# A band and strided attention feeding a GELU feed-forward layer: the start-up order written anew, with the residue mask and one exponential ahead of it

## The chip, the core and the metric

The kernel runs on one core of one Trainium2 chip. The core has a matrix engine (PE in the profile, with its weight loads as PEld), a vector engine (DVE), an activation engine (ACT), a general engine (POOL), a sequencer that issues the transfers (SP), and 16 DMA engines that carry them. The metric is the time of one launch in microseconds (us); less is better.

## The reference

Eight batches of eight heads, 576 tokens, head dimension 64. Heads 0 to 3 attend to a band of 32 tokens, heads 4 to 7 to all earlier tokens of the same residue modulo 32. The attention output, 4608 tokens of 512 channels, goes through a feed-forward layer with 2048 hidden units, all in float32:

```
rel = pos[:, None] - pos[None, :]
mask_local   = (rel >= 0) & (rel < 32)
mask_strided = (rel >= 0) & (pos[None, :] % 32 == pos[:, None] % 32)
scores = where(mask, (q @ k.T) / 8, -1e9)
attn   = softmax(scores);  x = attn @ v        # 4608 x 512
h = x @ w_in;  g = 0.5 * h * (1 + erf(h / sqrt(2)));  out = g @ w_out
```

## The kernel before

**Tiling.** The tokens are cut into 12 tiles of 384, the hidden units into 16 blocks of 128. One step n is one block for one tile: `ffn_h` (H of step n: 12 matmuls of 384 columns, lines 602 to 604), `ffn_g` (GELU and a cast on ACT, a subtraction on DVE, lines 611 to 615) and `ffn_o` (O of step n: 9 matmuls of 512 columns, lines 641 to 643). Every float32 product is made of three reduced ones, from a high and a low part of each operand: xh and xl of the tile, two parts of a weight block, gh and gl. There are 192 steps; steps 0 to 15 are those of tile 0, and tile 1 begins with step 16.

**Weights.** `load_w` brings block f as one transfer into a tile `ws`. `split_w` makes the two parts w from it in five pieces, which the order names with a c: a cast `lead` (line 150 on ACT or 148 on DVE, by `TOP_V`), an ACT piece (153), a DVE piece (155), the high part (161 on ACT or 159 on DVE, by `HIGH_V`) and the low part (163 on DVE).

**Attention of tile 0.** The band heads are three jobs L0 to L2 of 128 tokens (`local_job`: scores, a masked maximum on DVE at line 205, exponentials on ACT at 210, transposes, the product with v at line 263, and `to_x`, which writes xh on ACT at 230 and xl on DVE at 232). The strided heads of tile 0 are done on PE: two `half_tile` jobs (a and b; they need the residue mask `smask`, line 379) and one `strided_tile` job (A: line 413 on PE, four transposes on DVE at 418, casts on ACT at 421, subtractions on DVE at 424).

**Attention of tile 1.** The band heads are three jobs L3 to L5 (`band_job`): scores on PE (line 290), a masked maximum on DVE (304), exponentials on ACT (308), a normalization and a transpose on DVE (311 to 314), eight small transfers per job into a tile `first` (line 319, 16 KB each, issued by SP), the product with v on PE (328, written X_L) and `to_x`. The strided heads are done on DVE as "units" (u1): products of queries and keys, line 477, which come as a product and a read of its sum, and weighted sums at 517 and 519; their inputs are the tiles sq, sk and sv, loaded by the tokens E (sq and sk) and e (sv).

**What sets the order.** `START` lists the pieces up to step 15, one token per piece, and inside `manual_schedule` each of DVE, ACT, PE and SP runs its own pieces strictly in that order: w, q and v are loads of a weight block, of a job's queries and keys, and of its values; S and B load the strided inputs of tile 0 (qka and va); c, f, a, b, A and u advance a split, a step, a half tile, the strided tile, a unit; L advances a band job. POOL is not in that set: the scheduler orders its masks and fills. From step 16 on the order comes from `step(n)` and is the same in both kernels.

**Queues.** All transfers are issued by SP, in order. Each waits on the semaphore of the transfer eight places ahead of it, since eight semaphores go round; the first eight do not. So SP holds at most eight transfers in flight, and whatever stands behind one of them waits with it. A `first` transfer waits besides for the DVE transpose at line 314.

**Ahead of START** stand the masks on POOL (lines 691 to 712) and 50 small matmuls `lead_in` on zeros (line 684). The residue mask is made of four POOL instructions at line 712 and two DVE ones at 714 and 716, at the end of the masks.

Of the kernel before, what the change touches and what calls it, by code (L numbers as in the profile page):

```python
# [30 lines left out]
NGR = 16  # L31
# [19 lines left out]
    c0 c3 A0 w7 L2 A0 w5 L1 L2 L1 c3 c0 L3 L2 L1 v4 c0 A0 L1 L3 v5 c1 A0 L3 c3 f0 c1 w9 L3 c3 c1 c2 v3
    c3 c2 u1 c1 c4 f0 w6 c1 L4 w8 c2 f0 f1 c4 f0 c2 c7 w13 c4 c7 c2 f0 f1 c7 f1 c5 w14 f2 c4 e q5 c5 f1
    c4 f1 f2 c5 c7 u1 w10 f2 f3 c9 w11 c7 c9 L3 f2 f3 c5 f4 L3 c6 w12 f3 L3 c6 f3 f2 c5 f4 f4 c6 c8 w15
    f5 f4 c6 u1 c8 f3 c6 f5 c8 f5 c13 f6 f5 c13 c8 c9 f4 f6 f6 c8 c14 f7 f6 c14 c13 c9 c14 f5 c10 c9 c10
    f8 u1 f7 c10 f7 c13 f6 f7 c11 f8 f8 c13 f9 c11 f8 c10 c11 f7 c12 c10 c12 u1 f10 f9 c12 f9 c11 f9 f8
    L4 f10 f10 c11 u1 L5 f10 f9 c12 L4 L5 c12 f11 L5 u1 c14 L5 f10 f11 c14 f12 u1 f11 c15 f11 L4 L5 c15
    f13 u1 L5 f12 f12 L5 u1 f11 f13 f13 f12 f13 f14 u1 c15 f12 f14 f14 u1 c15 L4 f14 u1 f13 c15 L4 u1
    f15 L4 f14 f15 f15 f15 f15 f15
# [24 lines left out]
def attn_ffn_kernel(ctx: ExitStack, tc: tile.TileContext, qk, vl, qka, va, qs, ks, vs, w, out):  # L83
# [593 lines left out]


# [31 lines left out]
    for h in range(HL):  # L710
        m = smask[h * 32:(h + 1) * 32]
        nc.gpsimd.iota(m.bitcast(I32), pattern=[[-1, MA]], base=0, channel_multiplier=1)

    nc.vector.tensor_scalar(smask.bitcast(U32), smask.bitcast(U32), 0x80000000 | (STRIDE // NGR - 1), None,
                            ALU.bitwise_and)
# [201 lines left out]
```

## Time and profile before

| | |
|---|---|
| three timed runs | 881.61, 881.28, 881.52 us; median 881.52 us |
| the profiled execution | 880.11 us, of which 878.3 us are its span |
| PE busy in the span | 859.5 us of matmul, 771.0 us of weight loads |
| DVE, ACT, POOL busy | 704.0, 482.8, 17.4 us |
| mean granted PE clock | 0.992 |
| transfers | 66.67 MB, of which 16.8 MB are the 16 weight blocks |

A time in the profile counts from the start of the span. "Busy" is the sum of an engine's instructions, and the idle time before an instruction is put down to what released it. A tile's name carries no number in the profile, so H step 10 is the eleventh group of four instructions at line 602.

### The profile page before, as it was taken

What the parts mean: (1) busy time and instruction counts of PE and PEld (TensorE: products, weight loads), DVE (VectorE), ACT (ScalarE), POOL (GpSimd) and SP (SyncE); (2) the same over time, 40 slices, a digit from 0 to 9 for tenths busy, and PEclk for the clock granted to TensorE, in tenths of its full rate; (3) what the DMA queues carried; (4) which work ended last, traced back from release to release, by engine and by line L of the source; (5) the groups of instructions that cost most, each with busy time, mean ns of one, the idle gap of its engine ahead of it and who ended that gap; (6) DMA issues with size and microseconds to landing.
All of it is one profiled execution on the core that took longest, in us unless ns stands there. A gap on an engine that the chain in (4) does not pass through costs nothing.

```text
span 878.3 us, 19580 instructions
## 1 busy us (share of the span) xinstructions
PE 859.5 (98%) x6084; PEld 771.0 (88%) x6084; DVE 704.0 (80%) x4890; ACT 482.8 (55%) x990; POOL 17.4 (2%) x89
## 2 busy tenths in 40 slices
PE   7699999999999999999999999999999999999998
PEld 6598899989989989989998898988988988989997
DVE  5998899888898987798999979999799896751111
ACT  5898386259356357348547536636643743643222
POOL 5000100000000000000000000000000000000000
PEclk9699999999999999999999999999999999999999
DMA  9893220230220121121203112112012112000001
GB/s 311 302 387 121 87 79 19 82 110 20 82 82 15 60 91 58 34 79 39 86 3 114 33 57 85 44 51 106 19 56 90 41 34 65 9 11 7 29 1 37
DMA packets 34552, 66.67 MB, mean 76 GB/s; under 512 B 6800, under 2 KB 16528, under 8 KB 34448
## 3 DMA queue, kind: packets, MB, share of 16 engines
q1 hardware_dynamic: 34448, 65.43, 22.4%
q8 instruction: 48, 0.79, 0.4%
q14 instruction: 56, 0.46, 0.2%
HBM read 51.64 MB, written 9.44 MB: 70 GB/s over the span
## 4 chain that ended last, share of the span: by engine, by line
PE 95%; DVE 1%; POOL 1%; issue 1%; ACT 1%; SPq 0%; DMA 0%; POOLq 0%; ACTq 0%; DVEq 0%
PE H L602 16%; PE H L604 15%; PE O L642 15%; PE H L603 15%; PE O L643 15%; PE O L641 15%; PE X_L L328 2%; PE S_L L290 1%; SPq L319 0%; ACT PT_L L308 0%; PE S_L L254 0%; DVE w L163 0%; PE A L413 0%; DMA first<-PT_L 0%; POOL bmask L706 0%
## 5 line engine op out<-in xcount | busy, mean ns | idle before, releaser
L611 ACT ACTIVATE H<-H 128x384 f32<-128x384 f32 x192 | 91.3, 475 | 344.8 <-PE H L604 300.6
L602 PE MATMUL H<-xh,w 128*128 128x384 f32 x768 | 262.7, 342 | 1.2 <-ACT w L161 1.2
L604 PE MATMUL H<-xh,w 128*128 128x384 f32 x768 | 260.7, 339 | 0.9 <-DVE w L163 0.9
L603 PE MATMUL H<-xl,w 128*128 128x384 f32 x768 | 259.6, 338 | 0.6 <-DVE xl L424 0.6
L519 DVE SCALAR_TENSOR_TENSOR acc<-sv,sc,acc 128x64 f32<-128x64 f32 x1158 | 251.0, 283 | 0.5
L643 PE MATMUL O<-w,gl 128*128 128x512 f32 x576 | 228.2, 396 | 0.0
L642 PE MATMUL O<-w,gh 128*128 128x512 f32 x576 | 227.9, 396 | 0.0
L641 PE MATMUL O<-w,gh 128*128 128x512 f32 x576 | 224.6, 390 | 0.0
L477 DVE CUSTOM_DVE_ANT_0 junk<-sq,sk 128x64 f32<-128x64 f32 x1290 | 207.3, 224 | 2.7 <-issue 2.4
L615 DVE TENSOR_TENSOR gl<-H,gh 128x384 fp32r<-128x384 f32 x192 | 106.7, 556 | 109.8 <-ACT gh L613 109.6
L602 PEld LDWEIGHTS H<-xh,w 128*128 128x128 f32 x768 | 145.4, 189 | 10.7 <-ACT w L161 1.4
L603 PEld LDWEIGHTS H<-xl,w 128*128 128x128 f32 x768 | 145.1, 189 | 8.3 <-DVE xl L424 1.1
L604 PEld LDWEIGHTS H<-xh,w 128*128 128x128 f32 x768 | 145.1, 189 | 1.4 <-DVE w L163 1.4
L643 PEld LDWEIGHTS O<-w,gl 128*128 128x128 f32 x576 | 108.2, 188 | 23.1
L642 PEld LDWEIGHTS O<-w,gh 128*128 128x128 f32 x576 | 108.2, 188 | 18.0
L641 PEld LDWEIGHTS O<-w,gh 128*128 128x128 f32 x576 | 108.6, 189 | 17.4
L477 DVE DVE_READ_ACCUMULATOR2_ANT sc<- 128x1 f32 x1290 | 113.2, 88 | 0.0
L613 ACT CAST gh<-H 128x384 fp32r<-128x384 f32 x192 | 92.2, 480 | 6.0
L611 ACT ACT_TABLE_LOAD x60 | 77.0, 1283 | 1.1
L487 ACT ACT_TABLE_LOAD x35 | 44.9, 1283 | 0.6
L308 ACT ACTIVATE PT_L<-P_L,nm_L 128x64 f32<-128x64 f32 x132 | 44.3, 336 | 0.5 <-DVE nm_L L304 0.2
L308 ACT ACT_TABLE_LOAD x24 | 30.8, 1283 | 0.8 <-DMA band<-PT_L 0.3
(109 smaller groups left out, 489.6 us busy)
## 6 DMA issues: line engine op xcount, KB each, us to landing
ws<-in_w_dram SPq DMA_DIRECT2D x16, 1023.8 KB, 11.7
qk<-in_qk_dram SPq DMA_DIRECT2D x36, 320.0 KB, 4.6
out_dram<-ob SPq DMA_DIRECT2D x34, 256.0 KB, 2.6
vl<-in_vl_dram SPq DMA_DIRECT2D x36, 192.0 KB, 3.4
sk<-in_ks_dram SPq DMA_DIRECT2D x8, 576.0 KB, 4.9
sv<-in_vs_dram SPq DMA_DIRECT2D x8, 576.0 KB, 3.7
band<-PT_L SPq DMA_DIRECT2D x240, 16.0 KB, 1.8
sq<-in_qs_dram SPq DMA_DIRECT2D x4, 576.0 KB, 4.0
```

Of the source, the lines that this page charges most:

```text
L308: nc.scalar.activation(pv[:, :, h, :], p1[:, h * 2 * QB:(h + 1) * 2 * QB].rearrange("p (c t) -> p c t", c=2), AF.Exp, bias=nm[:, h:h + 1], ...
L477: nc.vector.tensor_tensor_reduce(junk, sq[vi, "q"][:, r0 + r, :], sq[vi, "k"][:, c, :], 1.0, 0.0, ALU.mult, ALU.add, ss[u][:, r, c:c + 1])
L519: nc.vector.scalar_tensor_tensor(acc[:, r, :], sq[vi, "v"][:, c, :], wgt, acc[:, r, :], ALU.mult, ALU.add)
L602: nc.tensor.matmul(hp, w1[f][:, 0, c, :], xh[:, c, :], start=(c == 0), stop=False)
L603: nc.tensor.matmul(hp, w1[f][:, 0, c, :], xl[:, c, :], start=False, stop=False)
L604: nc.tensor.matmul(hp, w1[f][:, 1, c, :], xh[:, c, :], start=False, stop=(c == NC - 1))
L611: nc.scalar.activation(hp, hp, AF.Gelu)
L613: nc.scalar.copy(gh, hp)
L615: nc.vector.tensor_tensor(gl, hp, gh.bitcast(F32), ALU.subtract)
L641: nc.tensor.matmul(o, gh[:, sl], w2[f][:, 0, :], start=(f == 0), stop=False)
L642: nc.tensor.matmul(o, gh[:, sl], w2[f][:, 1, :], start=False, stop=False)
L643: nc.tensor.matmul(o, gl[:, sl], w2[f][:, 0, :], start=False, stop=(f == NF - 1))
```

## The change

The list `START` is written anew, with other `TOP_V`, `HIGH_V` and `QUOT_V`. The residue mask moves from the end of the mask code to its head, on POOL and DVE. A tile `warm` of one column is zeroed by DVE, and ACT takes its exponential before anything else, so that the first table load of ACT stands there. The 50 `lead_in` matmuls become 18. The steps after 15 are not touched.

```diff
 START = """
-    q0 q2 S0 B0 q1 v0 v2 w0 L0 w3 v1 L2 L0 L0 L2 b0 q3 a0 L2 L0 b0 L0 b0 w1 b0 L0 a0 L1 L2 w2 a0 L2 a0
-    b0 L0 L1 a0 E b0 L0 w4 a0 L1 b0 L0 a0 b0 a0 b0 a0 b0 L2 L0 a0 c0 L1 q4 L2 b0 a0 L1 L0 c0 L1 A0 L1 L2
...
+    q0 q1 q2 S0 w0 w1 v0 B0 L0 v1 w3 L1 L0 L2 L0 L1 q5 L2 L1 L0 L0 L0 v2 b0 L2 L1 L1 a0 b0 b0 L1 L0 L2
+    b0 a0 L2 b0 a0 L1 L0 L2 w2 a0 L1 L2 b0 a0 c0 L2 a0 c0 b0 a0 b0 a0 q3 b0 a0 b0 c1 c0 w5 L0 a0 c1 b0
...
 """.split()
-TOP_V = [4, 6, 11]
-HIGH_V = [0, 2, 4, 5, 8, 12]
-QUOT_V = (1, 2)
+TOP_V = [0, 4, 5, 8]
+HIGH_V = [0, 2, 4, 5, 6, 13]
+QUOT_V = (0, 2)
...
+    for h in range(HL):
+        m = smask[h * 32:(h + 1) * 32]
+        nc.gpsimd.iota(m.bitcast(I32), pattern=[[-1, MA]], base=0, channel_multiplier=1)
+
+    nc.vector.tensor_scalar(smask.bitcast(U32), smask.bitcast(U32), 0x80000000 | (STRIDE // NGR - 1), None,
+                            ALU.bitwise_and)
+    nc.vector.tensor_scalar(smask, smask.bitcast(I32), 0, NEG, ALU.not_equal, ALU.mult)
+
+    warm = const.tile([P, 1], F32, name="warm")
+    nc.vector.memset(warm, 0.0)
+    nc.scalar.activation(warm, warm, AF.Exp)
 
     zero = const.tile([P, 32], F32, name="zero")
     nc.vector.memset(zero, 0.0)
     lead_in = ps_h.tile([P, TT], F32, name="lead_in", tag="H")
-    for i in range(50):
+    for i in range(18):
...
-    for h in range(HL):
-        m = smask[h * 32:(h + 1) * 32]
-        nc.gpsimd.iota(m.bitcast(I32), pattern=[[-1, MA]], base=0, channel_multiplier=1)
-
-    nc.vector.tensor_scalar(smask.bitcast(U32), smask.bitcast(U32), 0x80000000 | (STRIDE // NGR - 1), None,
-                            ALU.bitwise_and)
-    nc.vector.tensor_scalar(smask, smask.bitcast(I32), 0, NEG, ALU.not_equal, ALU.mult)
-
```

Three places show what the new list does. The first is SP's queue. Before, from the load of weight block 2 on (`ws_2`; the number behind a tile's name is its block or job, and the last number only counts tiles), these rows stand in it:

```order
L133 DMA ws_2_454<-in_w_dram 128x4095
L454 DMA sq_1_469<-in_qs_dram 128x256 x3
L454 DMA sk_1_473<-in_ks_dram 128x256 x3
L133 DMA ws_4_479<-in_w_dram 128x4095
L183 DMA qk_4_511<-in_qk_dram 128x640
L133 DMA ws_7_597<-in_w_dram 128x4095
L133 DMA ws_5_611<-in_w_dram 128x4095
L189 DMA vl_4_646<-in_vl_dram 96x512
L189 DMA vl_5_663<-in_vl_dram 96x512
L133 DMA ws_9_690<-in_w_dram 128x4095
L319 DMA first_0_283<-PT_L3_655 32x128 x8
L189 DMA vl_3_709<-in_vl_dram 96x512
```

Now, eleven weight blocks are issued first, and SP's queue goes on from the tenth and eleventh of them like this:

```order
L133 DMA ws_6_683<-in_w_dram 128x4095
L133 DMA ws_14_698<-in_w_dram 128x4095
L319 DMA first_2_258<-PT_L5_632 32x128 x8
L319 DMA first_1_256<-PT_L4_760 32x128 x8
L319 DMA first_0_254<-PT_L3_686 32x128 x8
L189 DMA vl_8_910<-in_vl_dram 96x512
L183 DMA qk_8_948<-in_qk_dram 128x640
L133 DMA ws_10_955<-in_w_dram 128x4095
L189 DMA vl_7_966<-in_vl_dram 96x512
L454 DMA sq_1_969<-in_qs_dram 128x256 x3
L454 DMA sk_1_973<-in_ks_dram 128x256 x3
L183 DMA qk_7_999<-in_qk_dram 128x640
```

All 24 `first` transfers stand together behind block 14; sq and sk of the units, which stood ahead of block 4, stand behind block 10, which itself stands behind the 24. Before, jobs L4 and L5 sent their 16 `first` transfers behind all weight blocks.

The second place is DVE ahead of step 0. Before, between the split of weight block 0 (tiles ws_0 and w_0) and the last xl of the band jobs:

```order
L155 SCALAR_TENSOR_TENSOR ws_0_306<-ws_0_306 128x1024
L418 STREAM_TRANSPOSE qka_0_295<-A0_0_387 128x256
L418 STREAM_TRANSPOSE qka_0_295<-A1_0_352 128x256
L418 STREAM_TRANSPOSE qka_0_295<-A2_0_523 128x256
L418 STREAM_TRANSPOSE qka_0_295<-A3_0_524 128x256
L159 CAST w_0_624<-ws_0_306 128x1024
L232 TENSOR_TENSOR xl_0_504<-S0_L2_325,xh_0_503 128x2x128
L163 TENSOR_TENSOR w_0_624<-ws_0_306,w_0_624 128x1024
```

Now, at the same place, DVE has:

```order
L159 CAST w_0_494<-ws_0_272 128x1024
L155 SCALAR_TENSOR_TENSOR ws_1_274<-ws_1_274 128x1024
L232 TENSOR_TENSOR xl_0_497<-S0_L0_279,xh_0_496 128x2x128
L163 TENSOR_TENSOR w_0_494<-ws_0_272,w_0_494 128x1024
L232 TENSOR_TENSOR xl_0_497<-S0_L1_296,xh_0_496 128x2x128
L163 TENSOR_TENSOR w_1_512<-ws_1_274,w_1_512 128x1024
L418 STREAM_TRANSPOSE qka_0_268<-A0_0_390 128x256
L418 STREAM_TRANSPOSE qka_0_268<-A1_0_351 128x256
L418 STREAM_TRANSPOSE qka_0_268<-A2_0_515 128x256
L418 STREAM_TRANSPOSE qka_0_268<-A3_0_516 128x256
L155 SCALAR_TENSOR_TENSOR ws_3_294<-ws_3_294 128x1024
L232 TENSOR_TENSOR xl_0_497<-S0_L2_313,xh_0_496 128x2x128
```

Blocks 0 and 1 are now both split before the strided transposes, and a piece of block 3 follows; before, block 1 was split only after the strided subtractions at line 424.

The third place is DVE around step 7, where the products of the units at line 477 (sc is their sum) now begin. Before, they began here, between the splits of blocks 3 and 1:

```order
L155 SCALAR_TENSOR_TENSOR ws_1_430<-ws_1_430 128x1024
L163 TENSOR_TENSOR w_3_704<-ws_3_321,w_3_704 128x1024
L477 ISA junk_3_3_0_719,sc_3_713<-sq_1_469,sk_1_473 128x64
L477 ISA sc_3_713 128x1
L477 ISA junk_4_3_0_721,sc_4_715<-sq_1_469,sk_1_473 128x64
```

Now they begin behind the low part of block 8, and this is where the first eight of them end:

```order
L477 ISA junk_4_3_1_1066,sc_4_1050<-sq_1_969,sk_1_973 128x64
L477 ISA sc_4_1050 128x1
L477 ISA junk_5_2_0_1068,sc_5_1052<-sq_1_969,sk_1_973 128x64
L477 ISA sc_5_1052 128x1
L155 SCALAR_TENSOR_TENSOR ws_10_955<-ws_10_955 128x1024
L615 TENSOR_TENSOR gl_7_1082<-H_7_1027,gh_7_1081 128x384
```

A piece of block 10 and gl of step 7 stand behind the eight products; 16 more products follow, and then the low part of block 10 (line 163).

More of the change, by code (lines that the diff above doesn't have):

```diff
@@ L48 @@
 START = """
-    q0 q2 S0 B0 q1 v0 v2 w0 L0 w3 v1 L2 L0 L0 L2 b0 q3 a0 L2 L0 b0 L0 b0 w1 b0 L0 a0 L1 L2 w2 a0 L2 a0
-    b0 L0 L1 a0 E b0 L0 w4 a0 L1 b0 L0 a0 b0 a0 b0 a0 b0 L2 L0 a0 c0 L1 q4 L2 b0 a0 L1 L0 c0 L1 A0 L1 L2
[L51 to L58, printed above, removed]
+    q0 q1 q2 S0 w0 w1 v0 B0 L0 v1 w3 L1 L0 L2 L0 L1 q5 L2 L1 L0 L0 L0 v2 b0 L2 L1 L1 a0 b0 b0 L1 L0 L2
+    b0 a0 L2 b0 a0 L1 L0 L2 w2 a0 L1 L2 b0 a0 c0 L2 a0 c0 b0 a0 b0 a0 q3 b0 a0 b0 c1 c0 w5 L0 a0 c1 b0
+    a0 q4 c0 L0 w7 c1 L1 L1 L0 c1 c0 A0 v4 A0 c3 L1 c1 c3 A0 L2 v5 L2 c3 w4 L5 A0 w8 L2 L5 c3 w9 A0 L3
+    c2 c3 c2 f0 w6 L3 L5 w14 c2 L3 L5 L4 f0 c2 f1 c5 c2 f0 c5 f0 L4 f0 f1 c5 f1 L4 c4 f2 c5 f1 c4 c5 L4
+    c7 f1 c4 f2 L3 f3 f2 c4 c7 f2 c4 f2 c6 c7 c6 f4 f3 c6 f3 c7 f3 L5 c6 c9 f3 c7 L5 c9 c6 f5 f4 L5 f4
+    c8 f4 c8 w10 L4 c9 E f5 f6 c8 L4 f5 c9 L4 f5 w11 f4 f6 c9 f6 c8 w13 f6 e f7 c10 c8 w15 w12 c10 u1 f5
+    v3 f7 c10 f7 c14 f8 f7 u1 c10 u1 c14 f6 f8 c10 c11 f9 u1 f8 c11 f8 u1 f7 f9 f9 c11 c13 f10 f9 c11
+    c14 c13 c11 f8 f10 c13 c12 f11 c12 c13 c13 f10 u1 f9 c12 f10 c12 u1 L3 f11 f10 c12 u1 f11 f12 L3 c14
+    f11 L3 u1 c15 f11 f12 c14 f12 c15 f13 f12 u1 c15 f12 f13 f13 u1 c15 f14 f13 u1 f13 f14 c15 f14 u1
+    f14 f15 u1 f14 f15 f15 f15 f15 f15
 """.split()
-TOP_V = [4, 6, 11]
-HIGH_V = [0, 2, 4, 5, 8, 12]
-QUOT_V = (1, 2)
+TOP_V = [0, 4, 5, 8]
+HIGH_V = [0, 2, 4, 5, 6, 13]
+QUOT_V = (0, 2)
 ROWS = [(vi, b, r) for vi, (b, r0, r1) in enumerate(VISITS) for r in range(r0, r1)]
```

## The prediction

> **What bounds the kernel now.** I read the chain of work that ended last first, then PE's waits, then PE's order of time, then stretches of the start.
>
> ```profile
> PE 95%; DVE 1%; POOL 1%; issue 1%; ACT 1%; SPq 0%; DMA 0%; POOLq 0%; ACTq 0%; DVEq 0%
> PE X_L L328 <- DMA first<-PT_L: 1.9, 1, 1.9
> 35.28 0.69 PE H L604
> 52.43 0.33 PE L602 MATMUL H<-xh,w 128*128 128x384 f32 x1
> 56.62 0.33 PE L602 MATMUL H<-xh,w 128*128 128x384 f32 x1
> 73.36 0.33 PE L602 MATMUL H<-xh,w 128*128 128x384 f32 x1
> 102.48 0.34 PE L602 MATMUL H<-xh,w 128*128 128x384 f32 x1
> ```
>
> 95% of the chain is PE. The third row, of the chain itself, is the third matmul of step 1. The four rows of matmuls are the first of H in steps 5, 6, 10 and 16: a step (H and one O) takes 56.62 - 52.43 = **4.19 us** when PE never waits. From step 16 on the order is the same in both kernels, and PE's only wait after that at 35.3 us is the 1.9 us for the `first` transfers of job L5, just ahead of step 13. So the time after step 16 is fixed, and the change is worth what it moves step 16, corrected for work that stands on the other side of it. Before, O of step 14 came behind H of step 16; in the changed order it comes ahead of it. O takes half a step, 2.1 us, so the moment to beat is 102.48 + 2.1 = 104.6.
>
> These are stretches of the start: the length, busy time and instructions of PE, PEld, DVE, ACT and POOL, the granted clock, the share of the DMA engines, GB/s.
>
> ```profile
> core 0: us, PE busy (x) PEld busy (x) DVE busy (x) ACT busy (x) POOL busy (x), PEclk, DMA share, GB/s
> 10.00:15.00 5.00, 2.93 (x39) 1.97 (x29) 3.19 (x19) 4.96 (x24) 3.15 (x15) 1.00 1.01 321
> 15.00:20.00 5.00, 4.60 (x92) 3.83 (x92) 4.52 (x18) 4.97 (x14) 0.00 (x0) 1.00 1.03 334
> 20.00:25.00 5.00, 2.76 (x125) 2.16 (x128) 4.31 (x9) 4.71 (x10) 0.00 (x0) 1.00 1.01 393
> 25.00:30.00 5.00, 4.16 (x37) 3.05 (x21) 4.47 (x17) 4.10 (x12) 0.00 (x0) 0.60 1.06 404
> 30.00:35.00 5.00, 1.69 (x34) 0.97 (x34) 5.00 (x21) 4.94 (x6) 0.00 (x0) 0.50 1.03 391
> 35.00:40.00 5.00, 4.72 (x14) 4.46 (x15) 5.00 (x7) 4.87 (x8) 0.00 (x0) 0.54 0.98 259
> 60.00:70.00 10.00, 10.00 (x52) 9.05 (x51) 9.77 (x27) 9.88 (x12) 0.00 (x0) 1.00 1.02 388
> ```
>
> The start has three limits at once: the DMA engines are full from 10 to 40 us, DVE has hardly an idle moment after 30, and the granted clock is half. Any plan has to bring 16.8 MB of weights through about 400 GB/s.
>
> **The front: masks, table, first steps.** Rows of DVE and ACT:
>
> ```profile
> 7.71 0.58 DVE L714 TENSOR_SCALAR smask<-smask 128x24 uint32<-128x24 uint32 x1 [6.82 <-POOL smask L712]
> 8.41 0.37 DVE L205 CUSTOM_DVE_ANT_0 pbig<-S_L,mask 128x96 f32<-128x96 f32 x1
> 8.90 1.28 ACT L210 ACT_TABLE_LOAD   x1 [8.90 <-DVE nm_L L205]
> 26.01 1.70 DVE L424 TENSOR_TENSOR xl<-qka,xh 128x192 fp32r<-128x192 f32 x4
> 31.11 1.22 DVE L163 TENSOR_TENSOR w<-ws,w 128x1024 fp32r<-128x1024 f32 x1
> 32.24 0.22 DVE L477 CUSTOM_DVE_ANT_0 junk<-sq,sk 128x64 f32<-128x64 f32 x1
> 33.40 0.69 DVE L148 CAST lead<-ws 128x1024 f16<-128x1024 bf16 x1
> 34.01 1.22 DVE L163 TENSOR_TENSOR w<-ws,w 128x1024 fp32r<-128x1024 f32 x1
> 35.14 1.22 DVE L155 SCALAR_TENSOR_TENSOR ws<-ws 128x1024 uint32<-128x1024 uint32 x1
> 81.95 0.46 DVE PT_L L314
> L615 DVE TENSOR_TENSOR gl<-H,gh 128x384 fp32r<-128x384 f32 x192 | 106.7, 556 | 109.8 <-ACT gh L613 109.6
> ```
>
> DVE sat 6.8 us for POOL's residue mask before it could touch the first scores at 8.41. With that mask first, it waits for POOL's band mask instead, which I put at 5.9 us, so 2.5 us sooner; the table load of 1.28 us goes from ACT's path. But H of step 0 needs the strided xl (line 424), which ended at 27.7, and the new order puts more ahead of it: two more pieces at line 155 and one more at 163 (1.13 us each from start to start, by 34.01 and 35.14) and a lead (0.61, 33.40 to 34.01), 4.0 us. DVE's idle time between 10 and 25 us was 2.98 us, of which I let 1.3 stay. 27.7 - 2.5 + 4.0 - 1.7 = 27.5; I take **28**. So the mask and the table by themselves start step 0 no earlier: their gain is spent on splitting blocks 1 and 3.
>
> What is gained is behind it. Before, step 1 waited for block 1 and ran its third matmul only at 35.3. Now block 1 is ready, and PE goes from step 0 to step 1 with the scores of L4 between. Then DVE is the limit: from 28 us to gl of step 2 its order holds six pieces at 155 or 163 for blocks 3, 2, 5 and 4 (6.8 us), three normalizations of four instructions (1.2 each, an estimate, of which line 314 has 0.46), two masked maxima (0.65 each, an estimate: four of 0.15 to 0.18), three high parts and two leads (0.6 each), and three gl (0.5 from start to start, 0.56 each): 16.2 us in all, so 44.3, with some small waits 44.5. O of step 2 ends near 46.5, H of step 4 at 48.6. With X of L5, O3, H5 and X of L4, step 6 begins at **54.2**, against 56.62.
>
> ```profile
> 47.61 0.62 PE X_L L328 x16
> 77.64 0.45 PE L290 MATMUL S_L<-qk 64*32 64x64 f32 x32
> ```
>
> By then one X (0.62) and one set of scores (0.45) more are done than before. The lead at step 6 is 2.4 + 0.6 + 0.45 = **3.5 us**.
>
> [...] These two rows of the chain are matmuls of one form, at a granted clock of 0.5 and of 1.0:
>
> ```profile
> 36.93 0.32 PE H L602
> 42.38 0.17 PE H L602
> ```
>
> [...] My sum has the clock half through step 0 and full in step 1; a cold step more costs 12 x 0.15 = 1.8 us, which the wait at step 10 below would take up for 1.3 us.
>
> **Transfers: the second limit.** The first row is the load of block 2, issued at 11.75; the others are SP's `first` issues, a later block behind one small load, and ACT's split piece.
>
> ```profile
> ws<-in_w_dram SPq DMA_DIRECT2D x1, 1023.8 KB, 13.9
> 30.14 12.70 SPq L319 DMA_DIRECT2D first<-PT_L  x8
> 82.43 10.71 SPq L319 DMA_DIRECT2D first<-PT_L  x16
> 43.51 2.19 SPq L133 DMA_DIRECT2D ws<-in_w_dram  x4
> ws<-in_w_dram SPq DMA_DIRECT2D x1, 1023.8 KB, 5.0
> 10.48 1.59 SPq L133 DMA_DIRECT2D ws<-in_w_dram  x2
> qk<-in_qk_dram SPq DMA_DIRECT2D x36, 320.0 KB, 4.6
> vl<-in_vl_dram SPq DMA_DIRECT2D x36, 192.0 KB, 3.4
> L153 ACT ACTIVATE ws<-lead x11: 1128/1149/1177, 18.1 to 57.8; 128x1024 int32<-128x1024 int16 x11
> 76.67 1.28 ACT L487 ACT_TABLE_LOAD   x1
> ```
>
> Block 2 landed at 11.75 + 13.9 = 25.7. The changed order has the very same 13 loads up to block 2, so I leave 25.7. Behind it come seven blocks, two qk and two vl, 8.39 MB; at 400 GB/s (the rows say 388 to 404) that is 21.0 us: block 14 lands at **46.7**. The eighth `first` of L5 waits for just that landing, as the eight of L3 did before (12.7 us for eight issues). From there SP needs 16 more `first`, and the row of 82.43 prices them: 10.71 us for 16, one short wait in it, so 0.64 each. 46.7 + 16 x 0.64 = 57.0; with vl_8 and qk_8, block 10 is issued at 58.1. Block 6 took 5.0 us from its issue with one vl ahead of it; with a qk more (0.8 us) block 10 lands at 63.9, and vl_7, sq and sk (0.98 MB, 2.5 us) at **66.4**.
>
> DVE meets sk at the first product of line 477 and stands there: by my count it is free at 60. Behind that product stand 7 more (all eight take 1.16 us, 32.24 to 33.40), a piece of block 10 (1.13), gl of step 7 (0.5), 16 products (2.3) and the low part of block 10 (1.13 to its start, 0.1 more): 66.4 + 1.1 + 1.13 + 0.5 + 2.3 + 1.2 = **72.6** for the third matmul of step 10. PE would have been there at 54.2 + 4 x 4.19 + 0.35 = 71.3: it waits 1.3 us. DVE goes on with 6 products, a maximum and subtraction per unit, gl 8, pieces at 155 of blocks 11 and 14, gl 9 and the low part of block 11: 6.1 us, 78.7, where PE stands at 76.8: 1.9 us more. Block 12 lands 4.9 MB behind sk (qk_7, four blocks, sv), near 78.4, and its split (two ACT pieces of 1.15, a gh, a table load of 1.28, three exponentials, the high and the low part) is done at 85.7, when PE is at its third matmul: 0.1. Neither of these waits was there before; the 1.9 us ahead of step 13 goes, since all `first` land by 59.
>
> **Sum.** 3.5 - 1.3 - 1.9 - 0.1 + 1.9 = **2.1 us** to the good. The profiled execution took 880.11 us, its span 878.3 and 1.8 around it; the changed one should take 878.0. It lies 1.4 below the median of the runs shown, 881.52, so on that scale I forecast **879.4 us**. A difference under 0.2% (1.8 us) a measurement of this kernel can hardly tell from no change, and mine is just above it.
>
> Unknowns, from both sides: a `first` at 0.58 to 0.68 moves sk by 0.8 us either way; block 14 at 404 GB/s throughout lands at 46.4, with five of its 21 us at 259 GB/s (as 35 to 40 us before) at 48.4. Instructions of the new table load at the head cost ACT nothing, since it had nothing to do before 8.9 us. The changed start has two table loads more on ACT (six against four up to step 11), 2.6 us, beside other work except the one priced above.
>
> That row of 1.28 is followed on ACT by the exponential at 77.97, with no more than 0.02 us between. [...]
>
> **Rivals.**
>
> *The waits for sk don't come* (24%). If SP issues the `first` faster, or the weights land earlier, by some 3 us together, steps 10 and 11 find their weights ready. For it: the order ahead of step 10 holds DVE back by nothing else. Against: 15 issues of 0.64 in a row. It would give 3.5 + 1.9 = 5.4 us: 876.1.
>
> *All transfers a little later, gain eaten* (20%). Block 14 at 48.4, or a colder PE: everything behind moves by 1.7 us, and the sum is 0.4: about 881.1, no change to be told. This is also where it ends if the planned order only moves waits from one place to another.
>
> *The tail of the weights comes late* (14%, slower). Blocks 10 to 12 with what lies between are 5.8 MB behind a queue that stood idle for 10 us, and PE's reserve at step 12 is 0.1 us. At 400 GB/s block 12 is there at 78.4; it breaks even with before at 350 GB/s (16.6 us, 2.1 later). At 300 GB/s, halfway to the 259 of one stretch, it lands 4.8 us later and costs 2.7 net: 884.2. For it: the new order has these four blocks far nearer to their use; before, all weights were in by 72 us. Against: 388 GB/s at 60 to 70 us.
>
> **How the numbers follow.** The forecast holds 42%, between 0.8 and 3.3 us of gain; a little over half of that lies above 1.8. Faster by over 0.2%: 24 + 23 = 47%; within: 19 + 20 = 39%; slower: 14%. The range reaches from the first rival, 876.1, to a slow tail of 1.4 us, 882.9, and leaves out the worse half of the slow case and the ends of the first.
>
> **What would show it.** In the profile after: the strided xl (line 424) ending near 28; H of step 1 following step 0 with no wait for w; 24 `first` in a row in SP's queue, the last 16 about 10 us long, ending near 57; DVE idle for several us near 60 to 66, ended by the transfer of sk; PE waiting for the low parts of blocks 10 and 11; no wait at X_L. If DVE has no such idle time, the first rival holds; if PE waits for block 12 or later ones by more than 2 us, the last. I would be wrong altogether if PE stopped in the first 50 us for something not in these lists, such as a 2 us wait of unknown cause.

## The result, and the profile after

| | before | after |
|---|---|---|
| timed runs | 881.57 us median (881.28 to 881.82, 4 runs) | 889.91 us median (889.36 to 891.66, 4 runs) |
| ratio, 95% interval | | 1.0100 [1.0087, 1.0113] |
| profiled execution, its span | 880.11, 878.3 us | 891.66, 889.9 us |
| mean granted PE clock | 0.992 | 0.981 |

The change makes the kernel 1.0% slower, outside the forecast range and on the other side. The chain of work that ended last, from the page of after, by engine:

```profile
PE 93%; DMA 5%; ACT 1%; SPq 0%; issue 0%; ACTq 0%
```

Before, DMA stood at 0% there; 5% of 889.9 us is some 45 us, and they lie ahead of 52 us, where the chain now goes through transfers almost without a break. The matmul that the prediction used as its mark, the first of H of step 16, from the timeline of after:

```profile
116.29 0.33 PE L602 MATMUL H<-xh,w 128*128 128x384 f32 x1
```

The moment to beat was 104.6 us. 116.29 is 11.7 later, and the span is 889.9 - 878.3 = 11.6 us longer: the whole loss lies ahead of step 16. The list of waits in the first 125 us of after (who waited for whom: us in total, times, longest) says where:

```profile
PE O L641 <- ACT gh L613: 10.9, 1, 10.9
ACT L308 <- DMA first<-PT_L: 10.7, 1, 10.7
DVE ss_L L311 <- ACT PT_L L308: 10.1, 1, 10.1
PE A L413 <- issue: 3.5, 1, 3.5
DVE qka L418 <- PE A L413: 3.3, 1, 3.3
PE S_L L254 <- issue: 2.2, 1, 2.2
```

One wait of 10.9 us on PE, of the same length on ACT and DVE, and two stops of PE that are put down to nothing ("issue"); a third, of 1.2 us, stands further down the list. None of these is in the prediction's lists. The chain from 31 us on, in order of time (start, us, what), shows the first one link by link:

```profile
31.35 18.24 DMA ws<-in_w_dram
...
49.61 1.71 DMA first<-PT_L
...
51.40 1.28 ACT L308
...
52.70 1.43 ACT PT_L L308 x8
54.13 1.02 ACT ws L153
...
55.17 1.18 ACT lead L150
...
56.37 1.28 ACT L611
...
57.66 0.48 ACT H L611
...
58.17 0.49 ACT gh L613
...
58.70 0.79 PE O L641
59.49 0.43 PE O L642
...
66.73 0.24 PE O L642
```

Weight block 14 lands at 49.6. The eighth `first` transfer of job L5, queued in SP eight places behind it, goes then and lands at 51.3. Only now does ACT load its table for the exponentials of job L4 (line 308); behind them stand two pieces of weight blocks, another table load, and the GELU of step 2, for which PE waits until 58.70. But why do exponentials wait for transfers that carry data *out* of SBUF? Line 296 answers: the tile PT, which the exponentials of a band job write and its `first` transfers read, has two buffers. The new list begins L5, then L3, then L4, so L4's exponentials write into the buffer that L5's transfers are still reading. From 45 to 50 us DVE and ACT do nothing at all, and from 50 to 60 PE is busy for 1.3 us (windows of after; columns as in the prediction):

```profile
45.00:50.00 5.00, 2.83 (x16) 2.38 (x14) 0.00 (x0) 0.00 (x0) 0.00 (x0) 1.00 0.44 161
50.00:60.00 10.00, 1.30 (x3) 1.11 (x4) 5.34 (x12) 8.46 (x16) 0.00 (x0) 0.53 0.04 10
```

The wait costs more than its 10.9 us. The granted clock falls during it, from 1.00 (45 to 50 us) to 0.50 (52 us), and stays there until 64 us, so that one matmul of O of step 2 takes 0.43 us where one of step 3 takes 0.24 (the last two rows of the chain): O of step 2 runs from 58.7 to 62.9, some 2 us longer than at the full clock.

The front was late too. Four rows of DVE in the timeline of after: the first masked maximum, a piece of block 0, the strided transposes, the strided xl:

```profile
6.03 0.26 DVE L205 CUSTOM_DVE_ANT_0 pbig<-S_L,mask 128x96 f32<-128x96 f32 x1 [3.95 <-POOL mask L709]
17.69 1.23 DVE L155 SCALAR_TENSOR_TENSOR ws<-ws 128x1024 uint32<-128x1024 uint32 x1 [2.21 <-ACT ws L153]
27.67 1.44 DVE L418 STREAM_TRANSPOSE qka<-A 128x256 f32<-128x256 f32 x4 [3.25 <-PE A L413]
31.05 1.71 DVE L424 TENSOR_TENSOR xl<-qka,xh 128x192 fp32r<-128x192 f32 x4
```

Mask and table did what was said (5.9 forecast), but the transposes waited 3.25 us for PE, and xl ended at 32.8 and not at 28. PE's other stop, 2.2 us at line 254, held up ACT's copy at line 256 for 1.9 us and, behind that, the piece of DVE at 17.69 for 2.2.

### The profile page after: what moved, and what is told of

Read it like the earlier page. It is cut to its first block, busy times and chain, and to the rows that moved or that the text cites. A ratio compares the mean times of both kernels' runs of the same rounds, so it can differ in the third digit from the quotient of the medians.

```text
span 889.9 us, 19445 instructions
## 1 busy us (share of the span) xinstructions
PE 861.0 (97%) x6020; PEld 771.8 (87%) x6020; DVE 705.7 (79%) x4892; ACT 484.7 (54%) x992; POOL 18.4 (2%) x89
## 4 chain that ended last, share of the span: by engine, by line
PE 93%; DMA 5%; ACT 1%; SPq 0%; issue 0%; ACTq 0%
PE H L602 15%; PE O L642 15%; PE O L643 15%; PE H L604 15%; PE H L603 15%; PE O L641 15%; DMA ws<-in_w_dram 2%; PE X_L L328 2%; DMA vl<-in_vl_dram 2%; DMA qk<-in_qk_dram 1%; PE S_L L290 1%; DMA first<-PT_L 0%; ACT PT_L L308 0%; ACT L611 0%; ACT L308 0%; SPq L183 0%
## 5 line engine op out<-in xcount | busy, mean ns | idle before, releaser
L519 DVE SCALAR_TENSOR_TENSOR acc<-sv,sc,acc 128x64 f32<-128x64 f32 x1158 | 248.1, 274 | 0.6
L641 PE MATMUL O<-w,gh 128*128 128x512 f32 x576 | 225.0, 391 | 10.9 <-ACT gh L613 10.9
L477 DVE CUSTOM_DVE_ANT_0 junk<-sq,sk 128x64 f32<-128x64 f32 x1290 | 204.7, 215 | 3.6 <-DMA sk<-in_ks_dram 3.5
L642 PEld LDWEIGHTS O<-w,gh 128*128 128x128 f32 x576 | 108.4, 188 | 18.3
L477 DVE DVE_READ_ACCUMULATOR2_ANT sc<- 128x1 f32 x1290 | 101.8, 79 | 0.0
L308 ACT ACT_TABLE_LOAD x25 | 32.1, 1283 | 11.2 <-DMA first<-PT_L 10.7
```

What stands on the lines that cost most here:

```text
L308: nc.scalar.activation(pv[:, :, h, :], p1[:, h * 2 * QB:(h + 1) * 2 * QB].rearrange("p (c t) -> p c t", c=2), AF.Exp, bias=nm[:, h:h + 1], ...
L477: nc.vector.tensor_tensor_reduce(junk, sq[vi, "q"][:, r0 + r, :], sq[vi, "k"][:, c, :], 1.0, 0.0, ALU.mult, ALU.add, ss[u][:, r, c:c + 1])
L519: nc.vector.scalar_tensor_tensor(acc[:, r, :], sq[vi, "v"][:, c, :], wgt, acc[:, r, :], ALU.mult, ALU.add)
L641: nc.tensor.matmul(o, gh[:, sl], w2[f][:, 0, :], start=(f == 0), stop=False)
L642: nc.tensor.matmul(o, gh[:, sl], w2[f][:, 1, :], start=False, stop=False)
```

## The experiments

The kernel before was measured again beside each group of them; its medians were 881.08 to 881.67 us, and the ratios are to these. Of each profiled execution, worked out from its records: when H of step 20 starts (to 0.2 us, since a few records are missing), how long PE idled until then, and how long it takes from there to the end. A profiled execution need not lie at the median: that of own_pt took 886.19 us, the longest of its nine, that of loads_behind 884.09, the longest of its seven, and that of lead18 880.08, the shortest of its ten. The medians decide which kernel is faster; the last three columns say where time went in one execution.

| kernel | median us | ratio to before, 95% | H of step 20 | PE idle before it | from it to the end |
|---|---|---|---|---|---|
| before | 881.57 | | 120.9 | 15.0 | 757.5 |
| after | 889.91 | 1.0100 [1.0087, 1.0113] | 132.2 | 25.1 | 757.7 |
| own_pt | 883.13 | 1.0028 [1.0017, 1.0040] | 126.8 | 19.5 | 757.6 |
| loads_behind | 882.45 | 1.0022 [1.0011, 1.0033] | 124.6 | 18.7 | 757.7 |
| mask_first | 880.90 | 1.0003 [0.9993, 1.0013] | 120.9 | 15.5 | 757.3 |
| lead18 | 884.82 | 1.0042 [1.0024, 1.0061] | 120.7 | 16.1 | 757.6 |
| lead18_again | 885.01, one run | | 125.8 | 18.4 | 757.5 |
| own_pt_lead50 | 884.29 | 1.0034 [1.0022, 1.0047] | 124.4 | 17.1 | 757.4 |
| own_pt_sk_early | 882.85 | 1.0015 [1.0006, 1.0024] | 123.6 | 18.3 | 757.4 |
| sk_early_lead34 | 884.20 | 1.0031 [1.0019, 1.0043] | 124.9 | 16.8 | 757.5 |
| sk_early_lead50 | 883.72 | 1.0025 [1.0015, 1.0036] | 124.9 | 17.4 | 757.4 |
| own_pt_sk_before_w14 | 883.03 | 1.0018 [1.0008, 1.0028] | 122.9 | 17.2 | 757.6 |
| sk_before_w14_lead50 | 883.37 | 1.0020 [1.0009, 1.0031] | 124.0 | 16.2 | 757.5 |
| weights_before_L3 | 882.86 | 1.0020 [1.0011, 1.0029] | 123.5 | 16.1 | 757.4 |
| gated_loads | 890.48, one run | | 131.0 | 24.4 | 757.7 |
| before_L5_sooner | 879.73 | 0.9978 [0.9968, 0.9987] | 119.4 | 12.9 | 757.4 |
| mask_first_L5_sooner | 880.04 | 0.9982 [0.9973, 0.9991] | 119.6 | 13.9 | 757.5 |

The last column is the frame for all that follows: from step 20 on, every kernel takes 757.3 to 757.7 us. What differs happens before.

### The buffer: own_pt and loads_behind

own_pt gives L4's tile PT a place of its own, in the room of sv:

```diff
-        p2 = lpool.tile([P, DM], F32, name=f"PT_L{x}", tag="PT", bufs=2)
+        if x == 4:
+            p2 = spool.tile([P, NR, D], F32, name=f"PT_L{x}", tag="sv", bufs=1).rearrange("p a d -> p (a d)")[:, 0:DM]
+        else:
+            p2 = lpool.tile([P, DM], F32, name=f"PT_L{x}", tag="PT", bufs=2)
```

> The changed kernel with one edit: the tile PT of band job L4 lies in the room of sv (not loaded before 76 us) and no longer in the buffer that L5's eight first transfers still read. Buffer theory (the 10.9 us in which PE stood ahead of O of step 2 came because L4's exponentials waited for L5's PT tile back): the wait of 10.7 us ahead of the table load at line 308 is gone, O of step 2 starts near 48 us and not at 58.7; the waits for sk and for the weights of steps 10 to 12, which the late PE had hidden, come back and eat 2 to 3 us, so 880 to 883 us. Front theory (the time was lost ahead of step 0, where PE stood 2.2 and 3.5 us for no named engine, and the half clock): step 0 stays at 31.9 us, PE waits at step 2 for something else, 887 to 890 us.

loads_behind leaves the buffer shared and makes it come free sooner:

```diff
-    ... c3 w9 A0 L3 c2 c3 c2 f0 w6 L3 L5 w14 c2 L3 L5 L4
+    ... c3 A0 L3 c2 c3 c2 f0 L3 L5 c2 L3 L5 w9 w6 w14 L4
```

> The changed kernel with one edit: the loads of weight blocks 9, 6 and 14 stand behind L5's eight first transfers in SP's queue, not ahead of them. Buffer theory: the eighth first waits for block 8 (landed at 41.7 us) and no longer for block 14 (49.6 us), so L5's PT tile is back near 43.4 us, L4's exponentials wait some 2.5 us and not 10.7, PE's gap ahead of O of step 2 falls from 10.9 to about 3 us: 881 to 884 us. Front theory: 887 to 890 us.

Rows of the timelines, first of own_pt (its lines stand three further down: 644 is 641 of after), then of loads_behind:

```profile
46.70 0.50 PE L644 MATMUL O<-w,gh 128*128 128x512 f32 x1 [0.21 <-ACT gh L616]
```

```profile
43.65 1.28 ACT L308 ACT_TABLE_LOAD   x1 [3.37 <-DMA first<-PT_L]
50.91 0.50 PE L641 MATMUL O<-w,gh 128*128 128x512 f32 x1 [3.59 <-ACT gh L613]
```

With its own buffer the wait is gone: 0.2 us is left ahead of O of step 2, which starts at 46.7 and not at 58.7. With the buffer shared but free sooner, the table load comes at 43.65 and not at 51.40, and PE's gap is 3.6 us and not 10.9. Both as the buffer theory had it; the front theory falls as the main cause. own_pt takes 6.8 us off the medians, a little less than forecast, and ends 2 us above before.

These rows of own_pt say how much of the forecast lead there is once the buffer is free: the strided xl, gl of step 2, and the first matmul of step 6.

```profile
29.70 1.71 DVE L427 TENSOR_TENSOR xl<-qka,xh 128x192 fp32r<-128x192 f32 x4
46.84 0.55 DVE L618 TENSOR_TENSOR gl<-H,gh 128x384 fp32r<-128x384 f32 x1
56.99 0.44 PE L605 MATMUL H<-xh,w 128*128 128x384 f32 x1
```

From the end of xl at 31.4 to the end of gl at 47.4 are 16.0 us, and the prediction's sum for this stretch was 16.2. But xl ends at 31.4 and not at 28, and step 6 starts at 56.99 and not at 54.2. By the prediction's own reckoning (before started it at 56.62, with 0.6 + 0.45 us less work done) that is a lead of 0.7 us and not of 3.5: the late front takes the rest. (O of step 2 can't be compared by itself. It starts at 50.35 in before, but H of step 4 and an X_L stand ahead of it there.) Then comes a new wait:

```profile
70.66 0.22 DVE L480 CUSTOM_DVE_ANT_0 junk<-sq,sk 128x64 f32<-128x64 f32 x1 [8.03 <-DMA sk<-in_ks_dram]
73.86 0.69 PE L605 MATMUL H<-xh,w 128*128 128x384 f32 x1 [4.06 <-DVE gl L618]
```

DVE's is the wait for sk which the prediction had named. PE's behind it is at another place than forecast: ahead of the first matmul of step 9, for gl of step 7, which stands behind the first eight products on DVE. In after, where everything is later, DVE waits 0.3 us for sk in the start, and PE not at all.

### The two other parts of the change alone: mask_first, lead18, lead18_again

mask_first is the kernel before with the residue mask's block and the exponential of `warm` moved ahead, lead18 the kernel before with one number changed:

```diff
-    for i in range(50):
+    for i in range(18):
```

> The kernel before with one part of the change: residue mask and the exponential of one column ahead of everything; list, 50 lead_in and the rest as before. If the front is bound by DVE: first masked maximum near 6.0 us and not 8.4, strided xl some 2 us sooner than 27.7, up to 2 us gained at the third matmul of step 1 (35.3), 879.5 to 881 us. If it is bound by the transfers or by PE's stops: the first maximum comes as soon, step 1 no sooner than 35, 881.5 us within 0.5. PE's stop of 2.2 us ahead of line 290 near 24.8 stays at the same instruction, since PE's program is the same.

> The kernel before with one part of the change: 18 lead_in matmuls and not 50; nothing else. Fetch theory (PE stops where it comes to the end of a block of 256 instructions while the next block is being fetched through full DMA queues; after: at PE's instructions 449 and 705, before: at 961): PE again stops at instruction numbers 193 + 256k, so 128 instructions later in the program than before; the stop of 2.2 us ahead of the scores at line 290 goes and one stands elsewhere. Rival (the stops belong to these instructions, by a wait that the profile doesn't name): the stop stays at line 290. Clock: if fewer warm-up matmuls leave the clock low for longer, stretches from 10 us on show a lower granted clock than before. Time by either 880 to 884 us.

> The kernel before with 18 lead_in matmuls, the same as lead18, for a second trace: its ten times ran from 880.1 to 888.1 us, and the one profiled was the lowest. If the spread comes from PE stopping at the ends of blocks of 256 instructions in some executions and not in others, a trace of a slow one (884 or more) shows a stop of 2 us or more for no named engine at instruction 449, 705 or 961 that the first trace did not have. If it comes from elsewhere (the clock, the transfers), it shows the same stops and a lower clock or later weights.

mask_first: the first masked maximum starts at 6.03 us, but xl (line 424) ends at 27.2, 0.5 sooner than before, and the third matmul of step 1 starts at 34.80 against 35.28. PE's stop at line 290 stays, at 1.8 us. No change is to be told in the time; the gain is not there to be spent.

```profile
25.56 1.68 DVE L424 TENSOR_TENSOR xl<-qka,xh 128x192 fp32r<-128x192 f32 x4
34.80 0.69 PE L604 MATMUL H<-xh,w 128*128 128x384 f32 x1 [0.97 <-DVE w L163]
```

lead18 is the surprise: 884.82 us at the median, between 880.1 and 888.1. The execution profiled first is the shortest of its ten and as fast as before. It has no stop at line 290 and none over 0.5 us elsewhere. Its granted clock is 0.66 from 10 to 20 us (half from 12 to 19), where before had 1.00, and 1.00 from 20 to 25 us, where after had 0.50 (windows of lead18):

```profile
15.00:20.00 5.00, 4.73 (x103) 3.90 (x111) 4.68 (x18) 4.97 (x14) 0.00 (x0) 0.61 1.03 368
20.00:25.00 5.00, 3.23 (x129) 2.21 (x129) 3.85 (x9) 3.98 (x10) 0.00 (x0) 1.00 1.06 389
```

The second trace, lead18_again, is of a longer execution, 885.01 us. The row of the strided products (line 413), first of lead18, then of lead18_again, with the window behind it:

```profile
21.02 0.38 PE L413 MATMUL A<-va 24*32 24x64 f32 x24 [0.43 <-issue]
```

```profile
25.47 0.50 PE L413 MATMUL A<-va 24*32 24x64 f32 x24 [3.37 <-issue]
25.00:30.00 5.00, 3.78 (x90) 2.85 (x89) 3.95 (x11) 2.93 (x8) 0.00 (x0) 0.50 1.04 384
```

Same program, same instruction, 0.43 us in one execution and 3.37 in another. Until step 20 PE idles 2.3 us more in the longer one, but H of step 20 is 5.1 us later: the other 2.8 us are PE's own time, with the clock at half in the products and scores behind the stop, which run at the full clock in the first trace. Stop and clock come together here, and no run parts them. That they are what makes lead18 slow in general is seen in one pair of traces only.

### PE's stops: own_pt_lead50, sk_early_lead34, gated_loads

The stops come at fixed numbers. Counting PE's matmuls, weight loads and semaphore instructions in a trace, the row behind the stop is number 450 (line 254) and 707 (line 413) in after, and 963 (line 290) in the kernel before, 257 and 256 apart. (Matmuls and weight loads alone, as the expectations count, give 446, 698 and 952.) The expectations call the three places 449, 705 and 961, and so does the text below. Rows of before and of after:

```profile
24.82 0.43 PE L290 MATMUL S_L<-qk 64*32 64x64 f32 x25 [2.16 <-issue]
```

```profile
15.65 0.38 PE L254 MATMUL S_L<-ident,P_L 128*96 128x128 f32 x2 [2.19 <-issue]
26.92 0.90 PE L413 MATMUL A<-va 24*32 24x64 f32 x40 [3.54 <-issue]
```

The trace also has transfers of kind "instruction" in 16 KB pieces on a queue of their own (48 of them, 0.79 MB, in before; called fetches below), and each of the stops at these places that is tabled below or shown here ends 2.3 to 2.8 us after such a transfer began. A lead_in matmul is four of the counted instructions (two matmuls and two weight loads), so 32 more of them shift the program by 128. own_pt_lead50 is own_pt with 50 lead_in matmuls; sk_early_lead34 and sk_early_lead50 are own_pt_sk_early (below) with 34 and 50.

> own_pt with 50 lead_in matmuls in place of 18, so that everything behind them stands 128 instructions later in PE's program (matmuls and weight loads counted). Fetch theory: PE stops for no named engine ahead of its instructions 449, 705 and 961 again, by number, which are now other places: the stops at line 254 near 15.6 us (2.3) and the one of 2.2 us late in the strided products (line 416) go; if one comes at 449 it is among the strided scores (line 373), at 705 earlier among the strided products, at 961 at line 290. Rival (the stops belong to these instructions): they stay at line 254 and late in line 416. If the stop in the strided products is what kept step 0 behind, step 0 starts 2 to 3 us sooner (28.5 to 30 us, own_pt about 30.5). Time 880 to 884 us, since DVE's wait of 8.0 us for sk then only grows.

> own_pt_sk_early with 34 lead_in matmuls, 64 instructions more ahead of all. Fetch theory: stops at PE's instructions 449 and 705 by number again, that is 64 instructions earlier in the work than with 18: at the end of the strided scores (line 373) and in the middle of line 416; none at line 254 near 15.6. Rival: stops stay at the same instructions. Time within 1.5 us of own_pt_sk_early by either.

> own_pt_sk_early with 50 lead_in matmuls. Fetch theory as in own_pt_lead50. If the clock and the stops of the front matter, step 0 starts 2 us sooner than in own_pt_sk_early and the time is 877 to 879 us; if the front is bound by DVE and the transfers, within 1 us of own_pt_sk_early.

The stops stayed with the numbers, not with the work. With 34 they stand at 449 among the strided scores (0.91 us), at 705 in the strided products (2.24) and at 961 (0.79); none at line 254. With 50 there is none at 449 or 705, but 1.9 to 2.2 us at 961, as before. (The stop of 1.2 us at line 290 in after is of another kind: with 34 it stands 64 instructions later, so it goes with the work. What it is stays open.) The row of own_pt_lead50:

```profile
27.10 0.65 PE L290 MATMUL S_L<-qk 64*32 64x64 f32 x25 [1.87 <-issue]
```

The times don't follow the number of stops, though: with 50 or 34 the medians are 0.3 to 1.4 us worse than with 18 in all four pairs (own_pt_lead50, at 884.29, just past the 884 expected), and though the intervals overlap in each, none goes the other way. Step 0 starts 1.2 us sooner in own_pt_lead50 than in own_pt but only 0.1 sooner in sk_early_lead50 than in own_pt_sk_early. gated_loads then holds weights back, by a small transfer that SP can't issue before job L0's xl is written:

```diff
+    def gate(x):
+        t = const.tile([P, 8], F32, name="gate")
+        nc.sync.dma_start(t, x_tile(0)[1][:, 0, 0:8].bitcast(F32))
...
-    ... v1 w3 L1 ... L2 w2 a0 ... q3 b0 ... c0 w5 L0 a0 ... a0 q4 c0 L0 w7 c1 L1 L1 L0 c1
+    ... v1 L1 ... L2 a0 ... b0 ... c0 L0 a0 ... a0 c0 L0 c1 L1 L1 L0 g w3 w2 q3 w5 q4 w7 c1
```

> own_pt with the loads of blocks 3, 2, 5 and 7 and two of queries held back in SP behind a small transfer that reads the xl of job L0 (written near 20 us), so that the DMA engines run empty for some us before it; weights come later, so the time is longer by several us and says nothing. Measured is the fetch of PE's next instructions. Theory (its packets queue behind the weight transfers): after PE passes its instruction 449 the next fetch comes within 3 us and not after 7.6, and PE does not stop at 705, or under 1 us. Rival (the fetch comes when PE is at the end of its block, whatever the transfers do): again 6 us or more after the passing of 449, and a stop of about 2 us at 705.

Its windows (the last two columns are the share of the DMA engines and GB/s) and its strided products, which run through 705 in one go:

```profile
15.00:20.00 5.00, 3.67 (x38) 2.79 (x37) 1.58 (x3) 3.15 (x4) 0.00 (x0) 0.50 0.61 165
20.00:25.00 5.00, 3.00 (x142) 2.46 (x140) 5.00 (x8) 2.50 (x4) 0.00 (x0) 0.50 0.15 32
```

```profile
22.56 1.92 PE L416 MATMUL A<-va 24*32 24x64 f32 x124 [1.77 <-DVE xl L232]
```

Where PE passed its instruction 449, when the next 16 KB fetch began, and the stop at 705:

```
                   449 passed   next fetch   later by   705 passed   stop there
before                 9.5         14.0         4.5        19.1        none
lead18                15.5         18.4         2.9        21.0        0.4
gated_loads           16.2         20.0         3.8        23.6        none
lead18_again          16.7         23.0         6.3        25.5        3.4
own_pt                15.6         23.2         7.6        25.6        2.2
after                 15.6         24.1         8.4        26.9        3.5
sk_early_lead34       11.9         22.3        10.4        24.9        2.2
```

In these seven executions the fetch that began 2.9 to 4.5 us after the passing of 449 went with a stop of at most 0.4 us at 705, and the one that began 6.3 to 10.4 us after it with a stop of 2.2 to 3.5. By these rows a stop looks like the wait for a fetch, and then it matters as well how soon PE gets from one of these places to the next: in after it passed 193 at 9.7 us, the fetch began at 13.0, but PE had run to 449 by 13.5 and stopped. That the weights hold the fetch up is less sure. With the DMA engines at 0.61 and 0.15 of their time and not full, it came after 3.8 us (under 3 expected) and not after the 7.6 of own_pt, and the stop went; that is one execution. But before and lead18 have full engines as well (a share of 1.01 from 10 to 15 us and 1.02 from 10 to 20), and there it came after 4.5 and 2.9. Why it begins 2.9 us later in one execution of lead18 and 6.3 in the other, with the engines full in both (388 and 367 GB/s), stays open.

### What keeps own_pt behind before: three more orders of SP's queue

own_pt_sk_early moves `E` (sq, sk) and `w10` behind L5's `first` transfers; own_pt_sk_before_w14 puts `E` in the place of `w14`, and `w14 w10` behind L4's transfers; weights_before_L3 puts `w10 w14 w11` there; sk_before_w14_lead50 is own_pt_sk_before_w14 with 50 lead_in matmuls. The diff is that of weights_before_L3 against own_pt:

```diff
-    ... w6 L3 L5 w14 c2 L3 L5 L4 f0 ... c4 c5 L4 c7 ... c8 w10 L4 c9 E f5 ... f5 w11 f4
+    ... w6 L3 L5 E c2 L3 L5 L4 f0 ... c4 c5 L4 w10 w14 w11 c7 ... c8 L4 c9 f5 ... f5 f4
```

> own_pt with sq, sk and weight block 10 loaded right behind L5's eight first transfers, ahead of the 16 of L4 and L3. Theory (SP's queue: sk and block 10 came 5 to 8 us late behind 16 issues of 0.63 us each): sk lands near 53 us and not 71.2, DVE's wait of 8.0 us for it and PE's of 4.1 us ahead of the third matmul of step 10 go, 878.5 to 880.5 us. Rival (DVE has no time left: without the wait the products only end up against another limit): PE waits for low parts of blocks 11 to 13 or at X_L instead, 882 to 884 us.

> own_pt with the loads reordered once more: sq and sk take the place of weight block 14 in SP's queue (ahead of L5's eight first transfers), blocks 14 and 10 stand behind L4's eight, ahead of L3's. Theory (in own_pt the waits for sk, in own_pt_sk_early the 4.0 us for L4's first transfers behind sk, sq and block 10, are the whole of what is left of the loss): sk lands near 47.5 us, L4's first transfers near 55, before PE wants them at 56.2, blocks 14 and 10 near 58; neither wait comes; H of step 16 starts near 103.6 us and not 107.6: 878.5 to 880 us, a little faster than the kernel before. Rival (each wait taken away only hands PE to the next one): another wait of 3 us or more between 60 and 105 us, 881.5 to 883 us.

> own_pt_sk_before_w14 with 50 lead_in matmuls. In the two pairs measured so far 50 in place of 18 cost 1 us at the median though the stops at instructions 449 and 705 went and one of 1.9 to 2.0 us at 961 came. If the number of stops were what counts, this is 1 us faster than own_pt_sk_before_w14; by the pairs it is about 1 us slower.

> own_pt_sk_before_w14 with blocks 10, 14 and 11, in this order, ahead of L3's eight first transfers (before: 14 and 10 ahead of them, 11 behind). Theory (the last wait of own_pt_sk_before_w14, 2.7 us of PE ahead of the third matmul of step 10, came because ACT stood 5.0 us for block 11, which landed at 73.8 us behind L3's transfers): block 11 lands near 63 us, PE's 2.7 us go, 880 to 881 us, within 0.1% of the kernel before. Rival (the loss that is left sits ahead of step 0, in PE's stops and the low clock, and the later waits only take up what PE has ahead): the wait goes, and the time stays at 882.5 to 883.5 us because another wait takes its place.

Each of the three orders took its wait away, and the times came out as the rivals had it (own_pt_sk_before_w14 at 883.03, just past its 881.5 to 883). With 50 lead_in matmuls, sk_before_w14_lead50 is 0.3 us slower at the median, too little to tell. own_pt_sk_early: sk lands at 54.5 and DVE doesn't wait for it, but L4's transfers stand behind block 10:

```profile
59.83 0.34 PE L331 MATMUL X_L<-first,vl 96*64 96x64 f32 x4 [3.60 <-DMA first<-PT_L]
```

own_pt_sk_before_w14: neither of these, but ACT stands for block 11 with a cast of H in step 8 behind it, and PE for that:

```profile
73.92 1.09 ACT L150 CAST lead<-ws 128x1024 f16<-128x1024 bf16 x1 [4.99 <-DMA ws<-in_w_dram]
76.03 0.45 PE L605 MATMUL H<-xh,w 128*128 128x384 f32 x1 [2.67 <-DVE gl L618]
```

weights_before_L3: no single wait over 1.1 us is left from step 0 on, and none took the place of the last one, yet the time is still 882.86:

```profile
86.11 0.50 PE L644 MATMUL O<-w,gh 128*128 128x512 f32 x1 [1.09 <-ACT gh L616]
87.49 0.50 PE L646 MATMUL O<-w,gl 128*128 128x512 f32 x1 [0.65 <-DVE gl L618]
```

Its PE idles 16.1 us before step 20, 1.1 more than in before; H of step 20 is 2.6 later. The other 1.5 us must be PE's own time. By the records, H and O until then take 0.4 us more than in before (85.8 and 85.4), the small matmuls of the attention the rest, though 32 lead_in matmuls are left out. The windows show what could make it: a granted clock of 0.50 from 20 to 25 us, where before had 1.00 (before is at 0.50 from 26 to 39 us and at 1.00 from 40 on), and 0.57 right behind the two waits above.

```profile
20.00:25.00 5.00, 1.84 (x88) 1.36 (x88) 4.82 (x7) 4.16 (x6) 0.00 (x0) 0.50 1.02 345
88.00:92.00 4.00, 4.00 (x14) 3.49 (x14) 3.42 (x18) 3.94 (x6) 0.00 (x0) 0.57 0.00 0
```

(The execution of before that was profiled is 1.4 us below its median, so these 2.6 are 1.5 between the medians.) So the residue is likely in the front, in waits of tenths and in the clock. No run tested the clock by itself.

### A version that beats both: before_L5_sooner

The kernel before has one late wait, 1.9 us for L5's transfers. In its list, L5's exponentials and normalization go ahead:

```diff
-    ... f9 c12 L4 L5 c12 f11 L5 u1 c14 L5 f10 f11
+    ... f9 c12 L5 L5 L5 L4 c12 f11 u1 c14 f10 f11
```

> The kernel before with its own last wait shortened: in the list, L5's exponentials come ahead of L4's and its normalization ahead of the split and the unit's sums. L5's first transfers start near 81 us and not at 82.4, so PE's 1.9 us ahead of X_L near 88.9 shrink to 0.4. If waits in the start count one for one, 879.5 to 880.3 us, some 1.5 below the kernel before; if another engine then is as late (the low part of block 11 or 12, now 1.3 us later on DVE), 881 us within 0.5.

> mask_first and before_L5_sooner together. mask_first alone changed nothing (0.9993 to 1.0013), since the third matmul of step 1 waits for the low part of block 1 all the same; so the same as before_L5_sooner within 0.5 us.

```profile
87.36 0.57 PE L328 MATMUL X_L<-first,vl 96*64 96x64 f32 x12 [0.79 <-DMA first<-PT_L]
```

879.73 us, 0.9978 [0.9968, 0.9987] of before and 10 us below after. The wait fell by 1.1 us, the medians by 1.9 [1.1, 2.8]: a wait here counts at least about one for one. With mask_first it is no better, as expected.

## Why the prediction was wrong, point by point

- **The time after step 16 is fixed.** Right: 757.3 to 757.7 us from step 20 on in all 17 traces.
- **Mask and table.** The instants were right, 6.03 us against 5.9, and so was the claim that by themselves they start step 0 no sooner: mask_first gains nothing.
- **The strided xl at 28.** Wrong by 4.8 us in after. The step let DVE's instructions set the time, with 1.3 us of idle time left, and took PE as ready. PE was not: its two stops, of 2.19 and 3.54 us, held DVE up for 2.2 (by way of ACT) and 3.25. In own_pt_lead50, without these two stops, xl ends at 30.2, behind a stop of 1.9 at another place. In own_pt it ends at 31.4, and that alone leaves 0.7 us of the forecast lead of 3.5 at step 6.
- **From 28 us to gl of step 2, 16.2 us of DVE work, "so 44.3, with some small waits 44.5".** This is the step that failed: gl ended at 59.2. Of these 14.7 us, 4.8 are the late xl and some 10 the wait of DVE for ACT. The sum counted DVE's work and left out what ACT needs in between, a free PT buffer for L4's exponentials, which came 10.7 us late. All the pieces were at hand: the eighth `first` of L5 waits for block 14 (the prediction says so itself and puts it at 46.7), and two buffers serve three jobs. It followed those transfers forward to X_L, their reader, and not back to the next writer of their source. The work itself was summed rightly: with the buffer free it takes 16.0 us.
- **Transfers.** Block 14 landed at 49.6 in after and 47.8 in own_pt (46.7 forecast, and 48.4 in the rival "all transfers a little later"). A `first` costs 0.63 us (0.64). The wait for sk exists, as own_pt shows, but was mis-sized and put at the wrong step: sk at 71.2 and not 66.4, PE 4.1 us ahead of step 9, for gl of step 7, and not 1.3 at step 10 for the low part of block 10. That gl stands behind the products was in the prediction's own list; that H of step 9 needs it was not. The wait at X_L goes in own_pt, as said.
- **lead_in.** Weighed by the clock alone: the prediction prices a step more at half the clock, 1.8 us by its two rows, and no row of it ties such a step to the number of lead_in matmuls. In after step 0 ran at half the clock (0.32 us from one matmul to the next) and step 1, but for its first matmul, at the full one (0.17), as its sum had it. With fewer lead_in matmuls the granted clock from 10 to 20 us was lower in one pair (0.66 in lead18, 1.00 in before) and higher in another (0.67 in own_pt_sk_early, 0.54 in sk_early_lead50). The 32 matmuls also shift which instructions stand at 449, 705 and 961. In the old order leaving them out costs 3.7 us between medians; the traces show a stop and a low clock together in a slow execution, so neither is refuted and neither shown alone. In the new order 18 is, if anything, better than 34 or 50, by 0.3 to 1.4 us at the median.
- **The rivals.** "The tail of the weights comes late" is there in own_pt in part: ACT stands 3.35 us for block 12 and PE 1.2 behind it, less than the 2 us named; in after the larger wait hides it. "The waits for sk don't come" came true in after (0.3 us), though because everything ahead was late: luck, and not its reason.
- **The table load.** The chain above has it again: 51.40, 1.28 us, the exponential at 52.70, with 0.02 us between as in the prediction's row.
- The last sentence said what would make it wrong altogether: a stop of PE in the first 50 us that is in none of the lists. That came, by name (10.9 us behind a buffer) and three times more without one.

## What to carry to other kernels

When a reorder moves a transfer that reads a tile, follow it both ways: to whoever reads what it writes, and to whoever next writes the buffer it reads; a buffer held by a queued transfer stopped ACT for 10.7 us here, and PE behind it for 10.9, and late data, sk in own_pt, stopped DVE for 8.0. A wait that disappears in a start limited by several things shows the next one, so price the second and third wait before the first one's gain is booked; here own_pt and the two orders tried next showed 4.1, 3.6 and 2.7 us, each at another place, and their medians lay within 0.3 us of each other.
